# Longformer attention with an MLP mixer on one core: the output stores of seven batches on GpSimd's queue, and the first gathered rows planned later on VectorE

## The chip, the cores and the metric

The kernel runs on one core of a Trainium2 chip. The metric is the device time of one execution in microseconds (us). Before the change three runs took 316.95, 317.31 and 317.64 us; the median is 317.31.

The core has five engines, each with its own stream of instructions that it takes strictly in order: PE (TensorE, matmuls; PEld is its weight load), DVE (VectorE), ACT (ScalarE), POOL (GpSimd) and SP (SyncE, which issues DMAs only). SP, ACT and POOL can issue DMAs; in the profile their issuing instructions stand under SPq, ACTq and POOL.

## The reference

B = 8 batches, H = 8 heads, S = 576 positions, D = 64, a window of 32 to each side, 8 global positions drawn at random.

```python
scores = scale * np.matmul(q, k.transpose(0, 1, 3, 2))
mask = np.abs(pos[:, None] - pos[None, :]) <= window
mask = mask | is_global[:, None] | is_global[None, :]
scores = np.where(mask, scores, -1000000000.0)
attn = softmax(scores); y = np.matmul(attn, v)              # (B, H, S, D)
x = y.transpose(0, 2, 1, 3).reshape(B, S, H * D)            # (8, 576, 512)
h = np.maximum(x.transpose(0, 2, 1) @ w_tok1, 0) @ w_tok2   # token mix, 256 wide
u = x + h.transpose(0, 2, 1)
out = u + np.maximum(u @ w_ch1, 0) @ w_ch2                  # channel mix, 1536 wide
```

q, k, v, the weights and out (8, 576, 512) are f32; the kernel computes in f16 with f32 accumulation.

## The kernel before, in words

The 576 positions are cut into four tiles of 128 and a rest of 64. For each batch the work goes through these stages; the line numbers are those of the profile.

- **Loads.** f32 tiles lq and lk (L504, two of 512 KB each), lr (the last 64 rows of q and k, L514) and lv (five chunks of v, L523). There is one tile of each, so the next batch's load must wait until the casts of this batch have read it. Batch 0 loads on SP, batches 1 and 2 on POOL, batches 3 to 7 with q, k on SP and v on ACT. They are cast to f16: qk (L534), rn (L531), vsh (L546), and vod is a shifted copy of vsh (L554).
- **Transposes.** For batches 0 to 2 on PE (copies of the result L569, L574, L587, L589); from batch 3 on by DMA on SP: rawr from rn (L639) and eight raw from qk (L643, turn_dma), which DVE copies into qT and kT (L646 to L654).
- **Global rows.** idx_i holds the row numbers of the global positions. An indirect DMA on POOL gathers these rows of q and of k (L487, f_gather), once for batches 0 to 3 and once for batches 4 to 7; L617 casts them (g_q, g_k).
- **Attention.** Scores in banks of PSUM (L673, with the mask of the global part added by a matmul at L666), exp into e (ACT, L683), the band mask (DVE, L689), global columns eg (L692), keys of the global rows (L703, lf L708 to L712), their sums (L720, rf L726), values (L740, L753), and x after the reciprocal (DVE, L780, L781).
- **Mixer.** Token mix (L803, L821, sum u on DVE at L834, ul for the rest of 64 rows), transposes of u (uT: PE at L848 for early batches, DMA at L853 later), first channel product (L866, relu into b by ACT at L858 or DVE at L860), second channel product (L895). DVE adds u into an f32 tile osb (L903), and the DMA at L906 stores it. The rest rows of two batches share one tile and are stored by the two DMAs of L909.

There are three osb tiles, used in turn: the add of a tile waits for the store of the tile three before.

The order of the work is not the order of the code. Each operation is recorded by op(engines with costs, priority, function, what it reads and writes, late=...), and a planner (run) then places all of them, one after the other, by priority, by the times at which it expects their inputs, and by its own table of costs. late adds to the time at which it expects a DMA to have landed, and so delays in the plan what reads the result; it puts no wait into the kernel. So a change of one cost or of one late re-orders instructions on all engines.

DMAs carry semaphores: those that SP and ACT issue use eight in turn (DMAHW0 to DMAHW7 in the listings below), and those of POOL eight of its own. An instruction that issues a DMA waits until the DMA that last used the same semaphore has landed.

Of the kernel before, what the change touches and what calls it, by code (L numbers as in the profile page):

```python
# [15 lines left out]
P = 128  # L16
# [11 lines left out]
def kernel(  # L28
# [12 lines left out]
    nc = tc.nc  # L41
    B, H, S, D = q.shape
# [49 lines left out]
    ENG = {"A": nc.scalar, "V": nc.vector, "G": nc.gpsimd, "S": nc.sync, "K": nc.scalar}  # L92
# [3 lines left out]
    def op(opts, pri, fn, r=(), w=(), ps=(), new=None, dma=None, mode="n", after=(), late=0.0, behind=()):  # L96

        i, deps = len(ops), set(after) | set(behind)
        for x in r:
            deps |= wrote.get(x, set())  # L100
        for x in w:
            deps |= wrote.get(x, set()) | read.get(x, set())
        for x in r:
            read.setdefault(x, set()).add(i)
        for x in w:
            wrote[x], read[x] = {i}, set()
        for x in ps:
            deps |= wrote.get(("ps", x), set())
            ps_uses.setdefault(x, set()).add(i)
            if opts[0][0] == "P":  # L110
                wrote[("ps", x)] = wrote.get(("ps", x), set()) | {i}
        deps.discard(i)
        ops.append(dict(opts=opts, pri=pri, fn=fn, deps=deps, ps=ps, new=new, dma=dma, mode=mode, late=late, behind=set(behind)))
        return i
# [192 lines left out]
    def qk_pads(i, eng):  # L307
        eng.memset(kTs[i][:, :, 0:WIN], 0.0)
        eng.memset(kTs[i][:, :, WIN + S :], 0.0)
        eng.memset(qTs[i][:, :, 0 : NT - 1, NG + P :], 0.0)  # L310
# [52 lines left out]
    g32 = [[const.tile([P, 2, D], F32, name=f"g32_{n}{t}") for t in range(2)] for n in "qk"]  # L363
# [71 lines left out]
    def f_pads2(i):  # L435
# [8 lines left out]
        out=gidx_r.rearrange("p g w -> p (g w)"), in_=bass.AP(tensor=gt32, offset=0, ap=[[0, 1], [1, 2 * NG]])), w=["gidx_r"], dma=(0.02, 64, 1.9, 1))  # L444
    op([("V", 0.1)], -195, lambda e: nc.vector.tensor_copy(out=gidx_h, in_=gidx_r[:, :, 0]), r=["gidx_r"], w=["gidx_h"])
    op([("P", 0.06)], -195, lambda e: nc.tensor.matmul(ps_tile["gx"], lhsT=ones, rhs=gidx_h, start=True, stop=True),
       r=["gidx_h"], ps=["gx"], new=("M", ["gx"], [P, NG], F32))
# [25 lines left out]
    def f_wc1(t):  # L473
        return lambda e: nc.gpsimd.dma_start(
            out=wc1[:, :, 512 * t : 512 * t + 512],
            in_=moe_w_ch1[:, 512 * t : 512 * t + 512].rearrange("(c p) x -> p c x", p=P),
        )
# [6 lines left out]
    def f_gather(t, ti):  # L484
        def f(e):
            for par in range(2):
                nc.gpsimd.indirect_dma_start(  # L487
                    out=g32[ti][t][:, par, :], out_offset=None, in_=rows[ti],
                    in_offset=bass.IndirectOffsetOnAxis(ap=idx_i[:, 2 * t + par : 2 * t + par + 1], axis=0),
                )  # L490
        return f

    TURN, STORE = (0.75, 256, 0.35, 544), (0.78, 2048, 0.8, 128)
# [393 lines left out]
    def chan2(b, tau, pri):  # L887
        i, key = b % 2, ("o", b, tau)
        last = tau == NT - 1
        js = [range(0, 4), range(4, 8), range(8, 12)] if b == 0 else [range(0, 6), range(6, 12)]  # L890
        for part, jr in enumerate(js):
            def f(e, jr=jr):
                for j in jr:
                    w = b1l[:, j, :] if last else b1[:, j, P * tau : P * tau + P]
                    nc.tensor.matmul(ps_tile[key], lhsT=w, rhs=wc2[:, j, :], start=(j == 0), stop=(j == NJ - 1))  # L895
            r = [("wc2", t) for t in sorted({j // 4 for j in jr})]
            r += [("b1l", t) for t in range(3)] if last else [("b1", j) for j in range(NJ)]
            op([("P", 0.2165 * len(jr))], pri - 0.5 * part if b else pri + 5 * part, f, r=r, ps=[key], new=("M", [key], [P, 512], F32) if part == 0 else None)
        o = nout[0] % 3
        nout[0] += 1  # L900
        osb = osbs[o]
        def g(e):
            nc.vector.tensor_add(out=osb, in0=uls[b // 2 % 2] if last else u16s[i][:, tau], in1=ps_tile[key])  # L903
        op([("V", 0.62)], pri - 8, g, r=[("ul", b // 2 % 2, 0), ("ul", b // 2 % 2, 1)] if last else [("u", i, tau)], ps=[key], w=[("osb", o)])
        if not last:
            op([("S", 0.45)], pri + 5, lambda e: nc.sync.dma_start(out=out[b, P * tau : P * tau + P, :], in_=osb), r=[("osb", o)], dma=STORE)  # L906
        else:
            for z in range(2):
                op([("S", 0.45)], pri + 5, lambda e, z=z: nc.sync.dma_start(  # L909
                    out=out[b - 1 + z, S - LAST : S, :], in_=osb[64 * z : 64 * z + 64]), r=[("osb", o)], dma=(0.39, 2048, 0.8, 64))  # L910
# [45 lines left out]
    for b in range(B):  # L956
        base = 100.0 * b
        ca = base - 85
        if b != 1:
            loads(b)  # L960
        if b == 0:
            n0 = len(ops) - 1
            op([("G", 1.0)], -176, f_w1, w=["w1"], dma=(1.7, 4096, 2.0, 512), behind=[n0])
            op([("G", 1.9)], -175, f_w1l, w=["w1l"], dma=(0.4, 4096, 2.0, 64), behind=[n0])
            n2 = len(ops) - 1
            op([("G", 0.77)], -173, f_wc1(0), w=[("wc1", 0)], dma=(2.6, 4096, 2.0, 512), behind=[n0])
            op([("G", 1.0)], -174.5, f_w2, w=["w2"], dma=(2.4, 4096, 2.0, 512), behind=[n0])
            for t in (1, 2):
                op([("G", 0.77)], -173 + t, f_wc1(t), w=[("wc1", t)], dma=(2.6, 4096, 2.0, 512), behind=[n0])
            n1 = len(ops) - 1  # L970
        if b == 1:
            op([("G", 1.2)], -18, lambda e: qk_pads(1, nc.gpsimd), w=[("qT", 1, p) for p in range(NP)] + [("kT", 1, p) for p in range(NP)] + [("qTr", 1), ("kTr", 1)], behind=[n1])
            op([("G", 1.7)], -17, f_pads(1), w=vall(1), behind=[n1])
            op([("G", 0.75)], -16, f_pads2(1), w=[("x", 1, NT - 1), ("lf", 1)])
        if b < 2:
            for ti in range(2):
                op([("G", 2.7)], (-115 if ti == 0 else -174.2) if b == 0 else 70, f_gather(b, ti), r=["idx"], w=[("g32", b, ti)], dma=(0.1, 256, 1.7, 256),
                   behind=[] if b == 0 and ti == 0 else [n2])
        casts(b)
        cast_v(b, ca - 20, [("A", 0.52), ("V", 0.57)] if b < 2 else [("A", 0.52)])  # L980
        shift_v(b, ca - 19, [slice(0, 2), slice(2, 4)] if b == 0 else [slice(0, 4)])
        if b == 0:
            loads(1, n0)
            op([("G", 0.77)], -40, f_wc2(0), w=[("wc2", 0)], dma=(2.6, 4096, 2.0, 512), behind=[len(ops) - 1])
            load_v(1, -39, [("G", 0.87)], [len(ops) - 1])
            n0 = len(ops) - 1
            for t in (1, 2):
                op([("G", 0.77)], -36 + t, f_wc2(t), w=[("wc2", t)], dma=(2.6, 4096, 2.0, 512), behind=[n0])
        if b == 1:
            glob_rows(0, slice(1, 4), ca - 40)  # L990
        if b == 4:
            glob_rows(1, slice(4, 8), 250)
        if b < PEB:
            rest_pe(b, ca - 38)
            for p in range(NP):
                turn_pe(b, p, ca - 37 + p)
            if b == 0:
                for pp in (slice(0, 1), slice(1, 2), slice(2, 4)):
                    glob_pe(b, pp, ca - 35 + pp.start)
            if b:  # L1000
                glob_cols(b, ca - 39)
        else:
            glob_cols(b, ca - 36)
            turn_dma(b, ca - 38)
        for p in range(NP):
            scores(b, p, ca - 30 + p)
        glob_keys(b, ca - 24 if b else ca - 18)
        glob_sums(b, ca - 20)
        for tau in range(NT):
            values(b, tau, ca - 15 + tau, b == 0)  # L1010
        token1(b, ca - 8)
        for tau in range(NT):
            token2(b, tau, ca + tau)
            if tau < NT - 1 or b % 2:
                turn_u(b, tau, ca + tau + 2, b < 3)
        if b and b % 2 == 0:
            chan2(b - 1, NT - 1, base + 24)
        for j in range(NJ):
            chan1(b, j, base + 20 + j)
        if b % 2:  # L1020
            for jj in range(3):
                chan1l(b, jj, base + 40 + jj)
        for tau in range(4):
            chan2(b, tau, base + 45 + tau)
        if b == B - 1:
            chan2(b, NT - 1, base + 50)
# [32 lines left out]
```

## Time and profile before

| what | value |
|---|---|
| median of the runs | 317.31 us |
| the profiled execution | 317.08 us |
| its span in the profile | 315.4 us |
| PE busy | 291.4 us (92%) |
| DVE busy | 187.6 us (59%) |
| ACT busy | 178.7 us (57%) |
| POOL busy | 44.5 us (14%) |
| mean granted PE clock | 0.984 |
| first and last store of L906 issued | 69.1 and 308.6 us |
| HBM read, written | 36.11 MB, 9.44 MB |

The first microseconds are loads, the making of masks and the first attention; from about 30 us on PE has work of several batches at hand, the mixer of one batch and the attention of the next. A row of the timeline gives start and length in us, engine, line, operation, output and inputs, how many instructions of the kind follow one another, and in brackets how long the engine had been idle before and what it had waited for.

### The profile page before, as it was taken

Reading aid. Unit: us, or ns where it says so; the run is one execution under the profiler, and the core shown is the slowest. Engines: PE = TensorE matmul, PEld = TensorE weight load, DVE = VectorE, ACT = ScalarE, POOL = GpSimd, SP = SyncE. Lnnn points to the kernel's source line nnn. Section 1 sums busy time; section 2 is a strip of 40 time slices with the busy share of each in tenths; the row PEclk is TensorE's granted clock in tenths of the full one; section 3 lists DMA queues with packets and bytes.
Section 4 is the critical chain, followed back from the end, with each engine's and each line's share of the span. In section 5 each row is a group of like instructions: output and inputs, shape, how many; then the busy total and the mean of one; then the engine's idle time right before and its main releaser. Section 6 shows DMA issues by size and latency. Waiting matters only on the chain.

```text
span 315.4 us, 7280 instructions
## 1 busy us (share of the span) xinstructions
PE 291.4 (92%) x2944; PEld 153.3 (49%) x2944; DVE 187.6 (59%) x413; ACT 178.7 (57%) x322; POOL 44.5 (14%) x81
## 2 busy tenths in 40 slices
PE   6968989997999898999999996799999999999993
PEld 3635645453474444444475443444465445444641
DVE  7588867569777587586675657772554257230021
ACT  4872895479996484965985693541832182305500
POOL 8588735620000000000000000000000000000000
PEclk9779999999999999799999999999999999999999
DMA  6999999999599979999999989415001401051013
GB/s 179 253 135 295 207 221 246 275 254 265 122 238 214 209 207 301 162 217 223 310 164 153 304 192 203 109 22 164 33 2 31 137 35 36 11 160 49 2 67 100
DMA packets 96452, 51.31 MB, mean 163 GB/s; under 512 B 73698, under 2 KB 89954, under 8 KB 96418
## 3 DMA queue, kind: packets, MB, share of 16 engines
q1 hardware_dynamic: 66512, 33.83, 48.7%
q0 software_dynamic: 6464, 11.11, 16.5%
q10 hardware_dynamic: 23442, 5.90, 9.9%
q8 instruction: 23, 0.38, 0.5%
q14 instruction: 11, 0.09, 0.1%
HBM read 36.11 MB, written 9.44 MB: 144 GB/s over the span
## 4 chain that ended last, share of the span: by engine, by line
PE 49%; DMA 24%; DVE 11%; ACT 10%; issue 2%; SPq 2%; ACTq 1%; POOL 0%; DVEq 0%
PE bank L895 19%; PE bank L866 16%; DMA raw<-qk 9%; DMA lq<-in_q_dram 5%; DMA g_q<-in_q_dram,idx_i 4%; PE bank L821 3%; ACT e L683 3%; PE bank L803 3%; ACT b L858 3%; DMA lk<-in_k_dram 2%; PE bank L673 2%; ACT qk L534 2%; PE bank L878 2%; DVE qT L569 1%; DMA lv<-in_v_dram 1%
## 5 line engine op out<-in xcount | busy, mean ns | idle before, releaser
L866 PE MATMUL bank<-uT,wc 128*128 128x512 f16 x384 | 93.3, 384 | 3.6 <-DVE qT L589 1.3
L895 PE MATMUL bank<-wc,b 128*128 128x512 f16 x384 | 87.8, 379 | 0.1
L858 ACT ACTIVATE b<-bank 128x512 f16<-128x512 f32 x86 | 50.9, 614 | 42.8 <-PE bank L866 36.9
L683 ACT ACTIVATE e<-bank 128x648 f16<-128x648 f32 x64 | 42.8, 730 | 35.0 <-PE bank L673 33.9
L895 PEld LDWEIGHTS <-b 128*128 128x128 f16 x384 | 36.9, 98 | 43.5 <-issue 0.4
L866 PEld LDWEIGHTS <-wc 128*128 128x128 f16 x384 | 35.3, 98 | 45.1 <-issue 6.9
L903 DVE TENSOR_TENSOR osb<-u,bank 128x512 f32<-128x512 f16 x32 | 21.7, 685 | 40.5 <-PE bank L895 40.2
L689 DVE TENSOR_TENSOR e<-e,masku 128x1296 f16<-128x1296 f16 x28 | 23.2, 830 | 17.0 <-ACT e L683 16.7
L546 ACT CAST vsh<-lv 128x512 f16<-128x512 f32 (+3 forms) x44 | 27.1, 620 | 5.2 <-DMA lv<-in_v_dram 4.1
L834 DVE TENSOR_TENSOR u<-x,bank 128x512 f16<-128x512 f16 x30 | 18.7, 682 | 13.1 <-PE bank L821 12.8
L781 DVE TENSOR_TENSOR x<-bank,rr 128x512 f16<-128x512 f32 x32 | 22.1, 691 | 1.1
L740 PE MATMUL bank<-rf,lf 128*64 128x264 f16 x144 | 15.1, 278 | 5.8 <-ACT b L858 2.0
L821 PE MATMUL bank<-a,w 128*128 128x512 f16 x80 | 19.9, 379 | 0.3 <-DVE a L809 0.2
L651 DVE COPY kT<-raw 128x512 f16<-128x512 f16 x20 | 12.0, 601 | 13.5 <-DMA raw<-qk 13.4
L803 PE MATMUL bank<-x,w 128*128 128x512 f16 x64 | 19.2, 387 | 0.5 <-DMA lq<-in_q_dram 0.4
L673 PEld LDWEIGHTS <-kT 64*128 64x128 f16 x576 | 11.6, 98 | 14.7 <-issue 13.9
L534 ACT CAST qk<-lq 128x512 f16<-128x512 f32 x26 | 15.9, 623 | 4.0 <-DMA lq<-in_q_dram 4.0
L534 ACT CAST qk<-lk 128x512 f16<-128x512 f32 x27 | 16.6, 625 | 2.6 <-DMA lk<-in_k_dram 2.6
L673 PE MATMUL bank<-qT,kT 64*128 64x72 f16 x576 | 15.9, 199 | 0.5 <-ACT e L683 0.4
L753 PEld LDWEIGHTS <-e 128*64 128x64 f16 x576 | 15.3, 111 | 0.2
L753 PE MATMUL bank<-vsh,e 128*64 128x66 f16 x320 | 15.3, 194 | 0.0
L654 DVE COPY qT<-raw 128x512 f16<-128x512 f16 x20 | 11.9, 601 | 4.8 <-DMA raw<-qk 4.8
(163 smaller groups left out, 321.2 us busy)
## 6 DMA issues: line engine op xcount, KB each, us to landing
out_dram<-osb SPq DMA_DIRECT2D x32, 256.0 KB, 2.5
lq<-in_q_dram SPq DMA_DIRECT2D x11, 512.0 KB, 6.2
lk<-in_k_dram SPq DMA_DIRECT2D x11, 512.0 KB, 7.6
lv<-in_v_dram ACTq DMA_DIRECT2D x15, 256.0 KB, 5.1
wc<-in_moe_w_ch_dram POOLq DMA_DIRECT2D x6, 512.0 KB, 12.6
lq<-in_q_dram POOLq DMA_DIRECT2D x4, 512.0 KB, 12.1
lk<-in_k_dram POOLq DMA_DIRECT2D x4, 512.0 KB, 10.1
lv<-in_v_dram ACTq DMA_DIRECT2D x10, 192.0 KB, 3.9
```

Of the source, the lines that this page charges most:

```text
L534: COPY[e](out=qk[:, ti, p].rearrange("q i (r d) -> q r i d", r=2), in_=(lq, lk)[ti][:, hs])
L546: COPY[e](out=vsh[i][a:z, c, :, 0:D], in_=lv[a:z, c])
L673: nc.tensor.matmul(ps_tile[keys[z]][:, u // 3, UW * (u % 3) : UW * (u % 3) + UW], lhsT=kT[r, 64 * u : 64 * u + P], rhs=qT[r, u // 2, UW * ...
L683: op([("A", 0.595)], pri + 1, lambda e, par=par: nc.scalar.activation(out=es[i][:, 2 * p + par].rearrange("p (n u) x -> p n u x", n=3), in ...
L689: op([("V", 0.85)], pri + 2, lambda e: nc.vector.tensor_mul(out=e2, in0=e2, in1=masku.unsqueeze(1).to_broadcast([P, 2, NB, UW])), r=["mask ...
L753: nc.tensor.matmul(o[:, VW * hh : VW * hh + VW], lhsT=es[i][:, h, 2 * tau + c, x : x + 64], rhs=vod[i][:, tau, h, :] if c else vsh[i][:, t ...
L781: nc.vector.tensor_tensor(out=xo, in0=pq[:, :, :, 0:D], in1=rr.unsqueeze(3).to_broadcast([P, 2, NP, D]), op=ALU.mult,)
L803: nc.tensor.matmul(ps_tile[key][:, tt], lhsT=w, rhs=x16s[i][:, ch, :], start=(ch == 0), stop=(ch == NT - 1))
L821: nc.tensor.matmul(ps_tile[key], lhsT=w2[:, ch, P * tau - sh : P * tau - sh + P], rhs=a1[:, ch, :], start=(ch == 0), stop=(ch == 1 and not ...
L858: nc.scalar.activation(out=out, in_=in_, func=AF.Relu)
L866: nc.tensor.matmul(ps_tile[key], lhsT=wc1[:, cc, P * j : P * j + P], rhs=uT[:, cc, :], start=(cc == 0), stop=(cc == 3))
L895: nc.tensor.matmul(ps_tile[key], lhsT=w, rhs=wc2[:, j, :], start=(j == 0), stop=(j == NJ - 1))
```

## The change

Two expressions change. The stores of L906 are issued on GpSimd (G) with the planner's cost for that queue, but for those of the last batch, which stay on SP (S). And the planner is told to expect the first gather (the q rows of batches 0 to 3) 2.3 us later.

```diff
-            op([("S", 0.45)], pri + 5, lambda e: nc.sync.dma_start(out=out[b, P * tau : P * tau + P, :], in_=osb), r=[("osb", o)], dma=STORE)
+            op([("G", 0.56) if b < B - 1 else ("S", 0.45)], pri + 5, lambda e: ENG[e].dma_start(out=out[b, P * tau : P * tau + P, :], in_=osb), r=[("osb", o)], dma=STORE)
...
-                op([("G", 2.7)], (-115 if ti == 0 else -174.2) if b == 0 else 70, f_gather(b, ti), r=["idx"], w=[("g32", b, ti)], dma=(0.1, 256, 1.7, 256),
+                op([("G", 2.7)], (-115 if ti == 0 else -174.2) if b == 0 else 70, f_gather(b, ti), r=["idx"], w=[("g32", b, ti)], dma=(0.1, 256, 1.7, 256), late=0.0 if b or ti else 2.3,
                    behind=[] if b == 0 and ti == 0 else [n2])
```

So 28 stores (seven batches of four) go from SP to POOL; the stores of L909 and the last four of L906 stay. The loads are on the queues that they were on. With the new plan, the order on the engines differs from the first batch on. Three places of it:

On DVE in the first batch, a piece of the difference; g_q is the cast of the gathered q rows (rows that did not change have no sign).

```order
@@ -49,5 +49,4 @@
 L534 CAST qk<-lk 128x2x4x64
 L692 COPY eg<-e_80 128x2x5x8
-L617 CAST g_q_195<-g_q_191 128x128
 L546 CAST vsh_76<-lv 32x8x64
 L546 CAST vsh_76<-lv 64x8x64
@@ -56,4 +55,5 @@
 L611 CAST kgz<-bank 64x2x8 x2
 L692 COPY eg<-e_80 128x2x5x8
+L617 CAST g_q_195<-g_q_191 128x128
 L554 COPY vod_78<-vsh_76 64x1056 x2
```

The cast went behind the two vsh casts, and behind the qT copies and kgz casts that stand ahead of the second eg.

On ACT where the loads and casts of a batch of the middle part stand (at about 118 to 126 us of the profile before). First before, then after; the brackets name the semaphores that an instruction waits for.

```order
L523 DMA lv<-in_v_dram 128x8x64 [waits DMAHW1_49,Activation_49]
L523 DMA lv<-in_v_dram 128x8x64 [waits DMAHW2_49,Activation_49]
L858 ACTIVATE b_100<-bank 128x512 [waits PE_49]
L523 DMA lv<-in_v_dram 128x8x64 [waits DMAHW5_49,Activation_49]
L531 CAST rn<-lr 128x512 [waits DMAHW3_49]
L534 CAST qk<-lq 128x2x4x64 [waits DMAHW4_49]
L858 ACTIVATE b_100<-bank 128x512 [waits PE_49]
```

After:

```order
L683 ACTIVATE e_81<-bank 128x648 [waits PE_49] x2
L523 DMA lv<-in_v_dram 128x8x64 [waits DMAHW2_49,Activation_49]
L523 DMA lv<-in_v_dram 128x8x64 [waits DMAHW3_49,Activation_49]
L858 ACTIVATE b_100<-bank 128x512 [waits PE_49]
L546 CAST vsh_76<-lv 32x8x64 [waits DMAHW7_49]
L546 CAST vsh_76<-lv 64x8x64
L546 CAST vsh_76<-lv 128x8x64
L531 CAST rn<-lr 128x512 [waits DMAHW4_49,DMAHW5_49,DMAHW1_49,Activation_49]
L534 CAST qk<-lq 128x2x4x64 [waits DMAHW6_49,Activation_49]
```

The last lv load stood between a relu and the casts and waited for the semaphore that an lk load of SP had used last (DMAHW5). Now two lv loads stand together behind the exps, on other semaphores, and the casts of rn and of qk come later.

On SP in the later part (at about 180 to 190 us of the profile before). First before, then after.

```order
L643 DMA_TRANSPOSE raw<-qk 128x4x128 [waits DMAHW6_49,Activation_49]
L643 DMA_TRANSPOSE raw<-qk 128x4x128 [waits DMAHW7_49,Activation_49]
L906 DMA out_dram<-osb_102 128x512 [waits DMAHW0_49,DVE_49]
L643 DMA_TRANSPOSE raw<-qk 128x4x128 [waits DMAHW1_49]
L643 DMA_TRANSPOSE raw<-qk 128x4x128 [waits DMAHW2_49,Activation_49]
L643 DMA_TRANSPOSE raw<-qk 128x4x128 [waits DMAHW3_49,Activation_49]
L906 DMA out_dram<-osb_103 128x512 [waits DMAHW4_49,DVE_49]
```

After:

```order
L853 DMA_TRANSPOSE uT<-u_0_94 128x4x128 [waits DMAHW4_49,DVE_49]
L504 DMA lk<-in_k_dram 128x4x256 [waits DMAHW6_49]
L504 DMA lq<-in_q_dram 128x4x256 [waits DMAHW7_49]
L504 DMA lk<-in_k_dram 128x4x256 [waits DMAHW0_49]
L639 DMA_TRANSPOSE rawr<-rn 128x4x128 [waits DMAHW1_49,Activation_49]
L643 DMA_TRANSPOSE raw<-qk 128x4x128 [waits DMAHW2_49,Activation_49]
L643 DMA_TRANSPOSE raw<-qk 128x4x128 [waits DMAHW3_49,Activation_49]
L643 DMA_TRANSPOSE raw<-qk 128x4x128 [waits DMAHW4_49,Activation_49]
L643 DMA_TRANSPOSE raw<-qk 128x4x128 [waits DMAHW5_49,Activation_49]
```

The stores between the transposes are gone from SP; the transposes of rawr and raw follow one another.

On DVE a little later (at about 192 to 200 us of the profile before), before and then after; rf and x are what the value matmuls of PE wait for.

```order
L903 TENSOR_TENSOR osb_104<-ul_97,bank 128x512
L654 COPY qT_73<-raw 128x4x128
L633 COPY qT_73<-gT 128x20x8
L651 COPY kT_75<-raw 128x512
L726 TENSOR_TENSOR rf_86<-bank,blk 128x528
L654 COPY qT_73<-raw 128x4x128
L651 COPY kT_75<-raw 128x512
L654 COPY qT_73<-raw 128x4x128
L780 RECIPROCAL rr_87<-bank 128x8
L781 TENSOR_TENSOR x_1_92<-bank,rr_87 128x512
```

After:

```order
L654 COPY qT_73<-raw 128x4x128
L903 TENSOR_TENSOR osb_104<-ul_97,bank 128x512
L726 TENSOR_TENSOR rf_86<-bank,blk 128x528
L651 COPY kT_75<-raw 128x512
L780 RECIPROCAL rr_87<-bank 128x8
L781 TENSOR_TENSOR x_1_92<-bank,rr_87 128x512
L780 RECIPROCAL rr_88<-bank 128x8
L781 TENSOR_TENSOR x_1_92<-bank,rr_88 128x512
```

rf moved ahead of a kT copy, and the x of all tiles ahead of the remaining copies of kT and qT.

## The prediction, on record before the changed kernel was run

> **What bounds the kernel now.** The views were read in this order: busy time in stretches of the span, the waits of TensorE (PE), then the rows of the timeline round each wait. The profiled execution took 317.08 us for a span of 315.4, 0.23 under the median of 317.31. First the stretches; the columns are window and length, busy time of PE, PEld, DVE, ACT and POOL with their counts, the granted PE clock, the DMA share and GB/s.
>
> ```profile
> 0.00:30.00 30.00, 22.50 (x330) 14.93 (x331) 22.85 (x84) 16.48 (x31) 23.75 (x54) 0.89 0.89 212
> 30.00:70.00 40.00, 38.53 (x400) 20.87 (x399) 27.64 (x58) 29.01 (x53) 20.72 (x28) 1.00 1.14 240
> 100.00:120.00 20.00, 18.83 (x168) 9.18 (x169) 15.25 (x30) 13.14 (x25) 0.00 (x0) 1.00 1.09 227
> 120.00:140.00 20.00, 17.99 (x174) 8.86 (x172) 13.62 (x33) 14.33 (x26) 0.00 (x0) 0.91 1.31 225
> 140.00:180.00 40.00, 39.92 (x392) 20.49 (x391) 27.36 (x53) 26.77 (x50) 0.00 (x0) 1.00 1.16 232
> 180.00:200.00 20.00, 15.20 (x234) 8.22 (x232) 11.90 (x27) 12.96 (x24) 0.00 (x0) 1.00 0.96 208
> 220.00:310.00 90.00, 90.00 (x782) 45.94 (x781) 33.17 (x64) 35.04 (x62) 0.00 (x0) 1.00 0.19 58
> ```
>
> From 220 us to the last tile PE never stops. So nothing that happens on another queue in the last third has a value, and the only way to an earlier end is to take PE's idle time, or its slow clock, out of the first 200 us. POOL computes nothing in 100 to 200 us (x0), so stores issued there displace no work of its own. PE's waits, for the stretches 18 to 35, 35 to 75, 75 to 130 and 180 to 230 us (total, times, longest; of the first two stretches the first row each):
>
> ```profile
> PE bank L666 <- DVE qT L569: 2.4, 2, 2.1
> ...
> PE bank L866 <- DVE qT L589: 1.3, 1, 1.3
> ...
> PE bank L740 <- ACT b L858: 2.0, 2, 1.3
> PE bank L866 <- DVE osb L903: 1.2, 1, 1.2
> PE bank L848 <- DVE u L834: 0.3, 1, 0.3
> ...
> PE bank L740 <- DVE x L781: 1.9, 1, 1.9
> PE bank L740 <- DVE rf L726: 1.4, 1, 1.4
> PE bank L720 <- DVE eg L692: 1.1, 1, 1.1
> PE bank L866 <- DMA uT<-u: 0.3, 1, 0.3
> ```
>
> The last seven, all between 75 and 200 us, add up to 8.2 us. Every term below is one of these rows or a clock row.
>
> **The change part by part.** *The first gathered rows.* The planner now puts the cast of the gathered q rows (L617) behind two vsh casts, two qT copies and more.
>
> ```profile
> 15.48 0.30 DVE L617 CAST g_q<-g_q 128x128 f16<-128x128 f32 x1 [1.70 <-DMA g_q<-in_q_dram,idx_i]
> 17.78 0.34 PE L666 MATMUL bank<-masko,ident 128*128 128x432 f16 x1 [2.15 <-DVE qT L569]
> ...
> 60.97 1.04 POOL L487 DMA_INDIRECT g_q<-in_q_dram,idx_i  x1 [1.47 <-DMA lq<-in_q_dram]
> 69.41 0.23 DVE L617 CAST g_q<-g_q 128x128 f16<-128x128 f32 x1 [1.80 <-DMA g_q<-in_q_dram,idx_i]
> 72.98 0.38 PE L866 MATMUL bank<-uT,wc 128*128 128x512 f16 x1 [1.33 <-DVE qT L589]
> ...
> q0 software_dynamic: 3889, 7.18, 96.5%
> ```
>
> VectorE (DVE) stood 1.70 us for that gather with ready casts behind it, and PE then stood 2.15 for qT. Removing it lets DVE, and PE with it, go on about 1.7 earlier at 18 us. What is late next is the second gather (batches 4 to 7): its cast at 69.41 waits 1.80, is not moved, and has the same casts and copies up to qT behind it, for which PE restarts at 72.98. That gather was issued on POOL at 60.97, where POOL itself waited for a load, and it landed some 8 us later among loads that fill the DMA engines: in 35 to 70 us the software queue alone took 96.5% of them (the q0 row). The loads are unchanged, so I take the restart at 73 us as set by them. The term lies between 0 and -1.7; I take 0, nearest to the 69.41 row, since an earlier PE then only waits longer.
>
> *The stall at 122 us.* Here the planner moves two lv loads on ACT ahead, behind exps, and the casts of rn and qk behind them.
>
> ```profile
> 78.66 0.34 ACTq L523 DMA_DIRECT2D lv<-in_v_dram  x1
> ...
> 121.98 2.06 ACTq L523 DMA_DIRECT2D lv<-in_v_dram  x1
> 124.08 0.62 ACT L531 CAST rn<-lr 128x512 f16<-128x512 f32 x1 [3.65 <-issue]
> 125.76 0.30 PE L740 MATMUL bank<-rf,lf 128*64 128x264 f16 x2 [1.31 <-ACT b L858]
> 126.77 0.30 PE L740 MATMUL bank<-rf,lf 128*64 128x264 f16 x2 [0.70 <-ACT b L858]
> ...
> 126.00:128.00 2.00, 1.30 (x32) 0.92 (x30) 0.68 (x3) 1.95 (x4) 0.00 (x0) 0.88 2.35 279
> 128.00:130.00 2.00, 2.00 (x6) 0.66 (x5) 1.30 (x4) 1.99 (x4) 0.00 (x0) 0.50 0.68 80
> 130.00:132.00 2.00, 2.00 (x9) 0.82 (x8) 0.77 (x2) 1.65 (x4) 0.00 (x0) 0.77 1.66 79
> ```
>
> An lv load that issues in 0.34 us elsewhere took 2.06 here, and ACT did no work for 3.65 us: the load waits for DMAHW5, the semaphore last used by an lk load of SP. The relus b behind it came late and PE stood 1.31 + 0.70 = 2.0. Then the clock dropped to half. Lost clock: 2 x (0.12 + 0.50 + 0.23) = 1.7 us. In the new order the two loads wait for semaphores whose earlier transfers are long over, so I take -2.0 and, since the slow clock followed the idle PE, -1.7. Both could stay (0) if the loads that SP issues land as late for another instruction.
>
> The clock row is weighed against one rule. The Trainium skill (TensorE: Matmul & The Clock Gate, Part 1: The HAM clock gate) says that PE falls to half clock after about 3.4 us of low activity, in windows that run free of the kernel. The trace agrees in level (0.50) but cannot show the windows. By that rule a gap at another place may cost the same again, and the forecast below would be 1.7 us later.
>
> *The stall at 186 to 200 us.* Stores and DMA transposes share SP's queue in before.
>
> ```profile
> 181.39 1.01 SPq L906 DMA_DIRECT2D out_dram<-osb  x2
> ...
> 183.82 0.69 DVE L903 TENSOR_TENSOR osb<-u,bank 128x512 f32<-128x512 f16 x1 [0.23 <-DMA out_dram<-osb]
> ...
> 188.20 0.60 DVE L651 COPY kT<-raw 128x512 f16<-128x512 f16 x1 [2.73 <-DMA raw<-qk]
> ...
> 194.45 0.60 DVE L651 COPY kT<-raw 128x512 f16<-128x512 f16 x1 [1.23 <-DMA raw<-qk]
> ...
> 197.71 0.60 DVE L651 COPY kT<-raw 128x512 f16<-128x512 f16 x1 [1.53 <-DMA raw<-qk]
> ```
>
> DVE takes its work in a fixed order, and three of its kT copies waited 2.73, 1.23 and 1.53 for raw transposes that SP issued behind stores. PE's waits of 1.1 (eg), 1.4 (rf) and 1.9 (x) in the table sit behind these copies: 4.4 in all. After, SP issues rawr and raw x4 in a row with no store between, and DVE has rf and the x's ahead of the last copies. That names the rf and x waits, 3.3, and most of eg. I take -3.5 and leave 0.9. Bounds: 0 (the copies stay late because their qk casts do) and -4.4.
>
> *Small ones.* PE's 1.2 for osb at 110 us: osb stood behind kT/qT copies; their order improves, but not wholly, -0.6 (0 to -1.2). The uT wait of 0.3 at 183 us: its transpose no longer stands behind stores, -0.3.
>
> *The 28 stores themselves.* SP loses 28 issues and POOL gains 28; DVE, ACT and PE lose nothing by it, except through the three osb buffers.
>
> ```profile
> L906 SPq DMA_DIRECT2D out_dram<-osb x32: 332/460/2318, 69.1 to 308.6; - x32
> L523 POOL DMA_DIRECT2D lv<-in_v_dram x10 | 8.6, 861 | 4.6 <-ACT b L858 1.6 <-DVE rr L780 1.2 <-issue 0.8
> 110.34 1.89 PE L866 MATMUL bank<-uT,wc 128*128 128x512 f16 x8 [1.17 <-DVE osb L903]
> out_dram<-osb SPq DMA_DIRECT2D x12, 256.0 KB, 3.6
> lv<-in_v_dram POOLq DMA_DIRECT2D x3, 256.0 KB, 10.8
> ```
>
> An issue took 0.46 on SP (median) and about 0.86 on POOL. SP landings took 3.6 us in 70 to 180 us; on POOL the nearest row is an lv load of the same size, 10.8, in the crowded 35 to 70 us. A buffer comes round after three tiles of 12 matmuls: at 1.89 per eight, 8.5 us. With 3.6 the store is done at 0.69 (the add) + 0.86 + 3.6 = 5.2 and nobody waits; with 10.8 it is 12.4, 3.9 too late. I take 3.6, because POOL's queue is empty after its loads have landed; the other end is a rival below. It may even gain: at 181.39 a store stood on SP for an osb written long before, and DVE waited 0.23 for it.
>
> *What the new order costs.* At 72 to 76 us ACT now has two lv issues ahead of g_k and kT work, which PE needs at once. Each costs 0.34 (78.66 row) to 2.06 (121.98 row): 0.7 to 4.1 for both; nearest is the near row, so +0.9. From there on the order differs on all engines, and waits will arise at places that before does not show. Bounds: 0, as nearly so in 140 to 180 us of before (39.92 busy of 40), and as many as before had in 75 to 200 us, 8.2. I take a third, +2.7: those 40 clean us are about a third of the stretch, and two of the other stalls are seen to be taken apart.
>
> Sum: 0 - 2.0 - 1.7 - 3.5 - 0.6 - 0.3 + 0.9 + 2.7 = -4.5. On 317.08 that is 312.6, and with the 0.23 of the median 312.8.
>
> **The rivals.** *The early gain carries (about 311.1).* If DVE, being earlier, releases what POOL waits for earlier, the gather lands earlier and the whole 1.7 survives. For it: POOL issues that gather late, after a wait of 1.47 for lq. Against: the 96.5% of DMA time, which no order of DVE changes.
>
> *Waits come back elsewhere (about 318).* All of 8.2 us of waits arises anew, as two schedules of one planner may be equally imperfect: 312.8 + 5.5 = 318.3, a little slower than before. For it: in the old trace each wait was an in-order engine behind one late transfer, and late transfers remain. Against: three of the places named are seen to be mended in the order. It decides as soon as new waits exceed 7.2 us. The Trainium skill (DMA: Bandwidth & Descriptors, Issuing engines are not separate DMA queues) speaks for it: transfers from any engine run on the same 16 DMA engines, and issuing from several saves only the issue time, usually small. No run here shows that yet; by it the stores' own part would be worth only the SP issue time.
>
> *Stores land late from POOL (about 326).* This is the one on the slower side. At 10.8 us to landing a buffer comes free 3.9 us late, DVE stands at L903 for it, and PE behind DVE for the bank. Batches have four such tiles, so the fourth meets the first: once per batch, in the three batches whose 12 stores fall in 70 to 180 us, 3 x 3.9 = 11.7, and the clock's 1.7 again: 312.8 + 13.4 = 326.2. It decides once a landing exceeds 8.5 - 0.69 - 0.86 = 6.9 us. Against: SP stores in the same stretch took 3.6 on DMA engines equally shared.
>
> **How the numbers follow.** A change under 0.2% (0.63 us) could not be told from none. The forecast (gain of 1 to 8 us) has 0.52, the early gain on top 0.12, waits elsewhere 0.29, late stores 0.07. The third scatters some 2 us round 318: 0.05 of it is faster by more than 0.63, 0.10 the same, 0.14 slower. So faster 0.69, same 0.10, slower 0.21. The low end, 309.0, is the forecast with hardly any new wait (312.8 - 2.7 = 310.1) and part of the early gain; about 0.04 lies below it. The high end, 319.0, takes in the waits elsewhere but for 0.08, and leaves out the late stores, 0.07.
>
> **What would show it.** Right: no PE wait for b (L858) and no clock below 0.9 near 125 us; PE idle in 180 to 200 us down from 4.8 to under 2; stores from POOL landing in 3 to 5 us and DVE's wait for out_dram at nearly nothing; the first g_q wait gone but the one near 69 us and PE's restart near 73 us as before; PE without a pause from about 196 instead of 200 us. Wrong: new PE waits of more than 7 us between 75 and 200 us, POOL landings above 6.9 us, a half clock at some other place, or a restart before 72 us.

## The result, and the profile after

Twenty runs of the changed kernel have a median of 314.97 us (310.92 to 317.82), twenty of the kernel before 317.28 us (314.01 to 320.16). The ratio is 0.9893, with a 95% interval of 0.9861 to 0.9925: about 3.4 us faster, where 4.5 had been forecast. Runs of one kernel differ by up to some 2%, and the ratios leave out those more than 1.5% above the fastest of their kernel, while the medians hold all. By the medians the gain is 2.3 us.

The profiled execution took 314.60 us (span 312.9) against 317.08. Its stretches, in the columns used above:

```profile
0.00:30.00 30.00, 24.71 (x338) 17.15 (x339) 24.21 (x88) 17.81 (x33) 24.14 (x54) 0.94 0.88 209
30.00:70.00 40.00, 37.06 (x390) 20.07 (x389) 26.26 (x54) 27.88 (x50) 20.91 (x29) 1.00 1.14 239
100.00:120.00 20.00, 17.79 (x156) 8.05 (x155) 13.67 (x28) 12.24 (x22) 1.77 (x3) 0.91 1.13 255
120.00:140.00 20.00, 19.66 (x188) 9.78 (x187) 13.97 (x33) 14.55 (x26) 0.00 (x0) 1.00 1.05 186
140.00:180.00 40.00, 37.79 (x376) 19.65 (x375) 28.62 (x55) 25.27 (x46) 3.58 (x6) 1.00 1.01 209
180.00:200.00 20.00, 19.16 (x255) 9.80 (x253) 13.02 (x31) 15.72 (x30) 1.08 (x2) 1.00 1.17 240
```

The idle PE time at 120 to 140 us (2.0 to 0.3) and at 180 to 200 us (4.8 to 0.8) is nearly gone. In its place there is idle time at 100 to 120 us (1.2 to 2.2), with the half clock that stood at 127 us before (0.91 has moved up a row), and at 140 to 180 us (0.1 to 2.2). PE's waits in 75 to 130, 130 to 180 and 180 to 230 us name one main cause for the new ones (rows of 0.4 us and less are left out in the second stretch):

```profile
PE bank L866 <- DVE osb L903: 2.3, 2, 2.1
PE bank L895 <- DVE osb L903: 0.4, 1, 0.4
...
PE bank L895 <- DVE osb L903: 1.8, 1, 1.8
...
PE bank L720 <- DVE eg L692: 0.8, 1, 0.8
```

It is the add that writes osb, late on DVE. At these places the store is not what it waits for. The timeline at the first of the two places:

```profile
109.65 0.62 DVE L654 COPY qT<-raw 128x512 f16<-128x512 f16 x1 [1.52 <-DMA raw<-qk]
...
112.03 0.59 DVE L654 COPY qT<-raw 128x512 f16<-128x512 f16 x1 [1.25 <-DMA raw<-qk]
112.54 0.68 DVE L903 TENSOR_TENSOR osb<-u,bank 128x512 f32<-128x512 f16 x1
...
113.27 1.85 PE L866 MATMUL bank<-uT,wc 128*128 128x512 f16 x4 [2.08 <-DVE osb L903]
```

The add stands behind qT copies, which wait 1.52 and 1.25 us for DMA transposes; it starts the moment that DVE is free, and PE, which needs the bank, stood 2.08 us. Now the stores, by issue on POOL and by landing in 70 to 180 us:

```profile
L906 POOL DMA_DIRECT2D out_dram<-osb x28: 540/540/857, 67.1 to 284.1; - x28
out_dram<-osb POOLq DMA_DIRECT2D x13, 256.0 KB, 5.2
```

They land in 5.2 us (median; SP's took 3.6), and no DVE instruction waits for one. But the first stores, issued between 67 and 75 us beside loads that still ran, took 7.2 to 10.3 us, and that the fourth add did not have to wait for the first of them was a matter of 0.1 to 0.2 us: the store was issued at 67.11 and landed some 7.2 later, and the add that takes its buffer again began at 74.45. The early part, at 15 and 70 us:

```profile
15.94 0.34 PE L666 MATMUL bank<-masko,ident 128*128 128x432 f16 x1 [0.18 <-DVE qT L569]
...
69.69 0.23 DVE L617 CAST g_q<-g_q 128x128 f16<-128x128 f32 x1 [2.06 <-DMA g_q<-in_q_dram,idx_i]
...
73.30 1.02 PE L866 MATMUL bank<-uT,wc 128*128 128x512 f16 x4 [1.62 <-DVE qT L589]
```

PE's wait of 2.15 us is down to 0.18 and it goes on 1.84 us earlier (15.94 for 17.78); but the second gather lands when it did, and PE restarts at 73.30 instead of 72.98.

### The profile page after: what moved, and what is told of

The parts are those of the page before. It is cut to its first block, busy times and chain, and to the rows that moved or that the text cites. A ratio compares the mean times of both kernels' runs of the same rounds, so it can differ in the third digit from the quotient of the medians.

```text
span 312.9 us, 7276 instructions
## 1 busy us (share of the span) xinstructions
PE 292.0 (93%) x2943; PEld 154.4 (49%) x2943; DVE 186.8 (60%) x410; ACT 180.5 (58%) x325; POOL 60.5 (19%) x109
## 4 chain that ended last, share of the span: by engine, by line
PE 58%; DMA 26%; ACT 5%; DVE 5%; issue 2%; SPq 2%; POOL 1%; POOLq 0%; ACTq 0%; DVEq 0%
PE bank L895 22%; PE bank L866 21%; DMA lv<-in_v_dram 8%; DMA raw<-qk 6%; DMA lq<-in_q_dram 5%; PE bank L821 4%; DMA g_q<-in_q_dram,idx_i 3%; PE bank L673 3%; PE bank L803 2%; DMA lk<-in_k_dram 2%; PE bank L878 2%; ACT qk L534 2%; ACT vsh L546 2%; DVE osb L903 2%; PE bank L753 1%
## 5 line engine op out<-in xcount | busy, mean ns | idle before, releaser
L858 ACT ACTIVATE b<-bank 128x512 f16<-128x512 f32 x88 | 52.5, 617 | 38.3 <-PE bank L866 38.3
L906 POOL DMA_DIRECT2D out_dram<-osb x28 | 16.1, 574 | 203.1 <-DVE osb L903 203.0
L753 PEld LDWEIGHTS <-e 128*64 128x64 f16 x576 | 16.1, 116 | 0.1
L753 PE MATMUL bank<-vsh,e 128*64 128x66 f16 x320 | 16.0, 199 | 0.0
```

Of the source, the lines that this page charges most:

```text
L753: nc.tensor.matmul(o[:, VW * hh : VW * hh + VW], lhsT=es[i][:, h, 2 * tau + c, x : x + 64], rhs=vod[i][:, tau, h, :] if c else vsh[i][:, t ...
L858: nc.scalar.activation(out=out, in_=in_, func=AF.Relu)
```

## The experiments

The two edits change an order and a queue together, but they can be taken apart. The planner's later time for the first gather moves, by itself, the cast of g_q some places back in DVE's order and takes out one warm-up matmul, and nothing else. And a store can be planned for one queue and issued on the other.

### One edit alone

The first, *e1*, keeps the stores on SP and has only the later gather.

```diff
-op([("G", 0.56) if b < B - 1 else ("S", 0.45)], ... ENG[e].dma_start(out=out[b, ...], in_=osb), ...)
+op([("S", 0.45)], ... nc.sync.dma_start(out=out[b, ...], in_=osb), ...)
```

> Only the planner's later time for the first gather; the stores stay on SP. On DVE the cast of g_q moves behind the vsh, qT and kgz work of the first batch, PE has one warm-up matmul fewer, and nothing else differs from the kernel before. Theory A (the gain is absorbed at the second gather): PE is about 1.7 us earlier at 18 us, restarts near 73 us as before (within 0.5), and the time is 317.3, within 0.6 of the kernel before. Theory B (the early gain carries and is half of the measured 3.4): 315.6, PE restarts near 71.3.

Measured: median 318.25, ratio 1.0028 (0.9981 to 1.0074). PE's restart after the second gather:

```profile
72.81 1.02 PE L866 MATMUL bank<-uT,wc 128*128 128x512 f16 x4 [0.98 <-DVE qT L589]
```

72.81, as before (72.98): theory A for this order, though the median lies 0.35 us above its range. The early gain is taken back by the second gather, and theory B (0.994) lies outside the interval.

The other, *e2*, has the stores on POOL and the cast of g_q where it was.

```diff
-dma=(0.1, 256, 1.7, 256), late=0.0 if b or ti else 2.3,
+dma=(0.1, 256, 1.7, 256),
```

> Only the stores of batches 0 to 6 planned and issued on POOL; the first gathered rows are cast where they were. All else is in the order of the changed kernel. Theory A: the time of the changed kernel, some 3.4 us under before (313.9), since the early part is worth nothing; DVE stands 1.7 for g_q at about 15 us and PE restarts near 73. Theory B: 315.6, half of the gain is lost.

Measured: median 318.97, ratio 0.9988 (0.9932 to 1.0045). Neither theory: without the late cast the changed kernel's order gains nothing. (Each ratio is to the kernel before on the same chip; the tests ran on several chips.) It was run again:

> e2 again, for a second look at it. If the early cast of the gathered rows costs this order time by itself: 316 to 319 again, at the same places (a stall near 15 us, then eg near 190 us). If e2 was chance of that chip: near the changed kernel, 313 to 315.

Median 319.97, ratio 0.9958 (0.9901 to 1.0016), while the changed kernel in a second test (*e6*) had 313.21 and 0.9869 (0.9834 to 0.9903):

> The changed kernel again, on the chip of the other runs of this call, to hold it against e2 and e4: 0.985 to 0.993 of before if its gain is real; 313 to 315 us.

Both medians lie above those of the kernel before on their chips (316.93 and 317.14), so it is hardly chance of a chip: in this order the place of one small cast at 15 us decides over some 1% of the time, though the interval of e12 overlaps those of the changed kernel. PE's wait for eg near 190 us was 0.8 and 0.9 us in the two profiles of the changed kernel; in e2 (a run of 316.87 us), and in e12 (one of 322.51), it was:

```profile
PE bank L720 <- DVE eg L692: 2.6, 1, 2.6
```

```profile
PE bank L720 <- DVE eg L692: 2.3, 1, 2.3
```

### Is it PE's clock?

The stall at 15 us may let PE's clock fall (the kernel before has the stall too, and 0.86 in the stretch shown here). The stretch from 16 to 28 us, with the granted clock third from the end, of e2 and of the changed kernel:

```profile
16.00:28.00 12.00, 9.28 (x163) 6.01 (x163) 9.04 (x23) 5.41 (x11) 11.33 (x16) 0.57 0.86 190
```

```profile
16.00:28.00 12.00, 10.23 (x179) 7.13 (x179) 10.33 (x30) 5.96 (x13) 11.10 (x16) 0.86 0.84 174
```

The mean clock over all runs agrees: 0.977 in e2 and 0.974 in e12, 0.989 in the changed kernel. *e13* is e2 with PE kept at work through that stall.

```diff
-    def warm(k, n):
-        for _ in range(n):
+    def warm(k, n, seen=[]):
+        for _ in range(n + (16 if seen.append(n) or len(seen) == 5 else 0)):
```

> e2 (the changed kernel without the later cast of the gathered rows) with 16 more warm-up matmuls on zeros at about 14.5 us, so that PE works through most of the stall that the early cast makes there; nothing else differs from e2, DVE's order least of all. Theory L (what the later cast is worth in this order is PE's clock: the stall at 15 to 17 us puts PE at half clock for about 10 us): 313 to 315.5 as the changed kernel, the half clock near 16 to 27 us is gone or 3.4 us long. Theory M (it is the order or the timing of DVE's work, not the clock): 316.5 to 319.5 as e2, with late eg at 190 us and osb at 112 us again.

Measured: median 318.61, ratio 1.0122 (1.0063 to 1.0181). Its clock in the stretch, and its wait near 190 us:

```profile
16.00:28.00 12.00, 8.45 (x171) 6.15 (x169) 9.53 (x23) 5.45 (x11) 11.10 (x17) 0.87 0.91 186
```

```profile
PE bank L720 <- DVE eg L692: 2.3, 1, 2.3
```

The early clock came up to 0.87, the median did not move, and eg is late again. By its median e13 is what theory M forecast. But the trace is of the fastest of its six runs, 314.83 us, which lies in theory L's range; the other five took 317.42 to 322.91 and left no trace. So neither the half clock at 16 to 28 us nor the late eg is shown to be what those runs lost. The half clock did not move PE's restart: it came at 72.56 us in e2, 73.30 in the changed kernel. Some lost clock goes with the loss all the same: of the 24 runs of e2 and e12 the six with a mean granted clock of 0.985 or more took 313.6 to 316.6 us, the sixteen below 0.980 took 316.9 to 323.5.

The traces do show one way from 15 us past the restart, and it leads through the stores. First the changed kernel, then e12:

```profile
67.11 0.59 POOL L906 DMA_DIRECT2D out_dram<-osb  x1 [1.65 <-DVE osb L903]
...
74.45 0.69 DVE L903 TENSOR_TENSOR osb<-u,bank 128x512 f32<-128x512 f16 x1
```

```profile
68.64 0.59 POOL L906 DMA_DIRECT2D out_dram<-osb  x1 [4.09 <-DVE osb L903]
...
78.58 0.69 DVE L903 TENSOR_TENSOR osb<-u,bank 128x512 f32<-128x512 f16 x1 [4.63 <-DMA out_dram<-osb]
...
79.32 1.87 PE L866 MATMUL bank<-uT,wc 128*128 128x512 f16 x4 [4.87 <-DVE osb L903]
```

With the late cast the first store is issued earlier (67.1 and 67.7 us in the two profiles of the changed kernel; 68.0, 68.6 and 67.9 in e2, e12 and e13), and it has landed when the fourth add needs its buffer. Without it this add waited 0.33, 4.63 and 0.59 us in the three traces, and in e12 PE ran at half clock from about 76.6 to 83.4 us. In the old order the fourth add comes at 76 to 77 us and waited in neither e4 nor e5 (below), which fits that the late cast is worth nothing there. Only e12's trace has the long stall; whether the other long runs stood at this place is not known.

### Order and queue taken apart

*e3* has the order of the changed kernel, with its stores issued on SP; *e4* has the order of the kernel before, with its stores issued on POOL.

```diff
 e3: changed kernel
-ENG[e].dma_start(out=out[b, ...], in_=osb)
+nc.sync.dma_start(out=out[b, ...], in_=osb)
 e4: kernel before
-nc.sync.dma_start(out=out[b, ...], in_=osb)
+(nc.gpsimd if b < B - 1 else nc.sync).dma_start(out=out[b, ...], in_=osb)
```

> The order of the changed kernel on PE, DVE, ACT and for SP's other DMAs, but the 28 stores are issued on SP where the plan had them on POOL. Theory C (the gain is the new order): 313.5 to 315, PE idle in 180 to 200 us under 2, the kT and qT copies of that batch wait under 1.5 each. Theory D (the gain is SP's queue without stores): 316.5 to 318, transposes behind stores land late and DVE waits over 2 us for raw at about 188 us.

> The order of the kernel before on PE, DVE and ACT; the 28 stores are taken out of SP's queue and issued on POOL. Theory C (new order): 316.5 to 317.5, the lv issue on ACT at 122 us still takes about 2 us and PE still waits 3 us or more in 186 to 200 us. Theory D (SP's queue): 313.5 to 315, PE's waits at 192 to 200 us fall from 4.4 to under 1.5 since raw lands earlier; the stall at 122 us stays.

e3 measured 319.38 (median), ratio 1.0098 (1.0054 to 1.0141): slower than before. e4 measured 314.77, ratio 0.9929 (0.9894 to 0.9964): the queue alone, with not one row of PE, DVE or ACT moved, gives about two thirds of the gain. On the time theory D has it, though not at every place it named. e3's stretches show why it is slow:

```profile
74.00:84.00 10.00, 6.89 (x59) 2.67 (x58) 4.56 (x8) 6.37 (x13) 0.00 (x0) 0.66 0.84 188
130.00:138.00 8.00, 6.22 (x41) 3.00 (x41) 2.65 (x9) 5.62 (x11) 0.00 (x0) 0.57 1.48 183
180.00:200.00 20.00, 19.96 (x180) 9.03 (x178) 13.58 (x27) 12.54 (x24) 0.00 (x0) 1.00 1.06 244
```

180 to 200 us is clean, which theory D did not expect; the time went at 74 and at 130 us, with half clocks of some 6.8 us each. At 78 us it is again the fourth add, which waits 1.75 us for the first store, here one on SP. And e4's:

```profile
120.00:140.00 20.00, 17.44 (x171) 8.61 (x170) 12.54 (x31) 13.72 (x25) 0.26 (x1) 0.91 0.99 198
180.00:200.00 20.00, 17.74 (x247) 9.27 (x246) 13.58 (x30) 14.35 (x26) 1.65 (x3) 1.00 1.19 222
```

The stall at 122 us stays (2.6 us idle), as both theories had it. At 180 to 200 us PE's idle time fell from 4.8 to 2.3: the queue alone takes half of that stall away, and the new order alone, by e3's row, all of it.

*e5* adds the late cast to e4 (the edit of the planner's number as in the change, on the old order).

> The old order with the stores issued on POOL (as in e4), and in addition the later cast of the first gathered rows. Theory E (that cast's early wait costs PE a half clock in many runs, whatever comes later): 313 to 314, the lost clock ((1 - granted clock) x time, mean over the runs) falls from the 5.4 us of e4 to about 3.5 to 4. Theory F (the late cast only shifts what comes behind it, and its worth is chance): within 1 us of e4, 313.8 to 315.8, or slower as in e1.

Measured: 314.51, ratio 0.9935 (0.9902 to 0.9967): e4 again. The mean clock rose as theory E says, from 0.983 to 0.990, and bought nothing that could be measured, so F on the time; at which places the runs without a trace had lost the clock is not known. The late cast is worth nothing in the old order, on either queue, and about 1% in the new one.

### What a store costs SP

In e7 a load of 64 bytes, and in e9 a copy of 64 bytes from osb, stands on SP where each store stood; the stores go by POOL as in e4. In e10 the tiny loads of e7 stand on ACT.

```diff
 e7, added beside each store
+nc.sync.dma_start(out=dum[0:1, 16 * z : 16 * z + 16], in_=q[0:1, 0, 0, 0:16])
 e9
+nc.sync.dma_start(out=dum[0:1, 16 * z : 16 * z + 16], in_=osb[0:1, 0:16])
 e10
+nc.scalar.dma_start(out=dum[0:1, 16 * z : 16 * z + 16], in_=q[0:1, 0, 0, 0:16])
```

> e4 with a load of 64 bytes of q into an unused tile on SP where each of the 28 stores stood: it takes the place in SP's queue, the issue time and the semaphore, and waits for no add. Theory G (a store holds SP up because it waits for the add on DVE): as e4, 314 to 315.5. Theory H (issue time and semaphores hold SP up): as before, 316.5 to 317.5. Theory I (the 256 KB of a store on the same queue hold the transposes up): as e4 too.

> As e7, but the 64 bytes are read from osb, so that SP also waits for the add as it did for the store; the 256 KB still go by POOL. Theory G: as before, 316.5 to 317.5, with PE's waits at 192 to 200 us back. Theories H and I: the same as e7 (as before under H, 314 to 315.5 under I).

> As e7 (old order, stores on POOL, 28 loads of 64 bytes), but the tiny loads are issued on ACT at the same place of the order: they take the eight semaphores in turn as before, and no place in SP's queue. Theory J (the semaphore turn is what the stores cost): as e7, 316.5 to 318, DMA waits of ACT and DVE in 75 to 205 us near 32 us. Theory K (the place in SP's queue): as e4, 314 to 315.5, DMA waits near 23.5; ACT's own extra issues, 28 x 0.35 = 10 us, lie in its idle time.

e7: median 317.80, ratio 0.9988 (0.9942 to 1.0035). e9: 322.57, ratio 1.0076 (1.0018 to 1.0134). e10: 323.97, ratio 1.0225 (1.0183 to 1.0266). A tiny load with nothing to wait for but its semaphore takes the gain of e4 away again by its median (the two intervals just overlap), as theory H has it; the bytes of the store (theory I) are not needed for that, nor the wait for the add (theory G). e9 and e10 came out slower than any theory had them. e9 is no clean test of G: its copies read osb and so keep the buffer, and the adds waited 2.8 us for them in 75 to 205 us. e10 shows the semaphore at work. Its ACT, in 75 to 205 us:

```profile
ACT e L683 <- DMA raw<-qk: 14.9, 2, 8.2
```

and the two places:

```profile
112.94 0.24 ACTq L906 DMA_DIRECT2D dum<-in_q_dram  x1
113.28 0.71 ACT L683 ACTIVATE e<-bank 128x648 f16<-128x648 f32 x1 [6.75 <-DMA raw<-qk]
...
151.42 0.73 ACTq L906 DMA_DIRECT2D dum<-in_q_dram  x2
152.25 1.31 ACT L683 ACTIVATE e<-bank 128x648 f16<-128x648 f32 x2 [8.17 <-DMA raw<-qk]
```

and PE behind the second of them:

```profile
153.02 0.70 PE L673 MATMUL bank<-qT,kT 64*128 64x72 f16 x17 [5.15 <-ACT e L683]
```

An exp reads no raw. It stands behind a load of 64 bytes that issues in 0.24 us, once the transpose that last used its semaphore has landed. Not all of the idle time is the load's: at the first place the scores were only written by 110.79 us, so the load held the exp for some 2.5 us of the 6.75; at the second they were there at 146.33, the exp came 5.9 us later, and PE stood 5.15 us for it. In the kernel before, the lv load at 121.98 likewise stood 1.55 us before it was issued (ACT's last work ended at 120.43); why its issue then took 2.06 us, these runs don't show. So the turn of eight semaphores can be a cost of every DMA on SP and ACT, whoever issues it; that it is the larger part of what e7 lost, and not the issue time on SP, was not separated, since e10 pays its price on a busier engine.

### One step on

What is left in the changed kernel are adds behind qT copies that wait for raw. *e11* tells the planner that raw lands later, so that it puts the copies further back.

```diff
-r=[("qk", ti, p)], w=[("raw", ti, p)], dma=TURN)
+r=[("qk", ti, p)], w=[("raw", ti, p)], dma=TURN, late=2.5)
```

> The changed kernel with one more number for the planner: the DMA transposes of raw are expected 2.5 us later, so that DVE has the adds into osb ahead of more of the kT and qT copies. If the two new PE stalls behind osb (2.1 us near 112 and 1.8 near 141) are what is left of the old ones, the first falls under 1 us, the second stays, and the time is 1 to 2.5 us under the changed kernel, 311 to 312.5. If other waits take their place: 312.5 to 316.

Measured: median 312.94, ratio 0.9837 (0.9796 to 0.9878), the lowest of all here, though its interval overlaps that of the changed kernel in its second test (0.9834 to 0.9903). The time falls just into the second of the two ranges, that of other waits in their place. The waits for osb of 75 to 130 us:

```profile
PE bank L895 <- DVE osb L903: 0.4, 1, 0.4
PE bank L866 <- DVE osb L903: 0.2, 1, 0.2
```

and the only wait in 180 to 230 us:

```profile
PE bank L866 <- DMA uT<-u: 2.4, 1, 2.4
```

Both stalls behind osb went (the second had been expected to stay), and part of their time came back as waits for ACT's relus and for uT.

## Why the prediction was right, and where its steps were not

The time, the sign and the size came out: 4.5 us forecast, 3.4 measured, inside the range. That the size is so near is in part luck: with what the profiles show for each term (the rows below) the sum is -1.8, and the two profiles lie 2.5 us apart. Step by step:

- *PE is the bound and only idle time before 200 us counts.* Right: PE is busy throughout 200 to 220 us after as before, and the end moved by 2.2 us in the profiles (last add 310.45 to 308.22), less than the clearing of 180 to 200 us alone.
- *The early term, 0.* Right where it was argued: the restart stood at 73.30 for 72.98, and e1 and e5 show nothing gained. Its reason, that what lies ahead of the second gather is covered, holds for the restart, also under half clock (e2), but not for the first store, which is issued ahead of it. What the step missed is that the same edit decides about 1% once the order behind it has changed (e2 and e12 against the changed kernel).
- *The stall at 122 us, -2.0 and -1.7.* The wait of 2.0 went as described, but the clock's 1.7 did not: 15 us earlier PE stood 2.08 us for osb, and the half clock came there. The term that failed beside it is the small one, -0.6 for osb at 110 us: that wait grew from 1.2 to 2.3. It had been seen that the add stands behind qT copies, but not that one of them waits for a later transpose in the new order.
- *The stall at 186 to 200 us, -3.5.* Right in size: PE's waits there fell from 4.4 to 0.8. Both causes named, SP without stores and DVE's order, do it: e4 shows half from the queue alone, e3 nearly all from the order alone.
- *The 28 stores on POOL.* Right, in the changed kernel's profile, that nobody waits for them. Issue took 0.54 (0.86 taken), landing 5.2 in the middle part (3.6 taken), short of the 6.9 from which the late-store rival decides. But the step looked at 70 to 180 us only. The first stores took 7.2 to 10.3 us, above that limit, and without the late cast the add waited for one, 4.63 us in e12: the rival that had 0.07 is real at this one place.
- *New waits, +2.7, and 72 to 76 us, +0.9.* The restart cost 0.3. In 75 to 200 us PE's waits are 6.1 us after against 8.2 before; without osb at 110 and eg, 3.0 are new. Of some 6.2 us of waits that went, 4.1 came back, with the half clock: the rival "waits come back elsewhere" described about two thirds of what happened.
- *The Trainium skill's two rules.* Of its page TensorE: Matmul & The Clock Gate (Part 1: The HAM clock gate) the traces bear out that half clock comes in stretches of some 3.4 us: 127.5 to 130.9 before, 113.3 to 116.7 after. A gap elsewhere did cost the same again, as that rule allowed. Of the Trainium skill's page DMA: Bandwidth & Descriptors (Issuing engines are not separate DMA queues), no run here tests the first half. By its second half, that another issuer saves only issue time, usually small, e4 would have gained next to nothing. It gained 0.7%. A DMA that leaves SP leaves a place in an in-order queue and a turn of the semaphores; e7 does not part the two.

## What to carry to other kernels

Ask of a DMA not only how long it takes but what it stands in front of: its place in an in-order queue, and its semaphore, which a later DMA must wait for. A store that nobody waits for belongs on a queue with nothing behind it. Where a planner writes the order, change the queue and the order apart, as in e3 and e4: here the new order with the late cast, but with the stores on SP, was 1% slower, the queue alone 0.7% faster, and all together 1.1% to 1.3% faster. And look at the first stores by themselves: the landing time of the middle part said nothing about those that meet the loads.

## What was not expected of the hardware

A load of 64 bytes on ACT held an exp up for 5.9 us, through a semaphore shared with SP's transposes. And PE at a granted clock of 0.57 for 12 us, early in e2, did not delay its restart after the second gather (72.56 us against 73.30 in the changed kernel).
